# Packing the attention outputs of six head groups: an output projection with six products instead of eight

## The chip, the core and the metric

The kernel runs on one core of a Trainium2 chip. The metric is the device time of one execution in microseconds; less is better. The engines of the core are TensorE (PE, matrix products, with weight loads shown as PEld), VectorE (DVE), ScalarE (ACT), GpSimd (POOL) and SyncE (SP), which here mostly issues transfers.

## The reference

One transformer layer on a sequence of 2048 rows of 640 columns, in bf16: layer norm, attention with 32 heads of 20 columns each, an output projection with a residual, then layer norm and a bilinear gated feed-forward part of 1728 columns with a residual.

```
qkv = layernorm(x) @ wqkv                      # 640 -> 3 x 32 heads x 20
p   = softmax(q @ k.T * 20**-0.5)              # per head, 2048 x 2048
h   = x + concat_heads(p @ v) @ wo             # wo: 640 x 640
g   = layernorm(h) @ w_gate;  u = layernorm(h) @ w_up      # 640 -> 1728
out = h + (g * u) @ w_down
```

## The kernel before

**Layout.** The 32 heads are held in eight groups of four (NG = 8, HPG = 4). Each head has a slot of 32 partitions (SLOT), of which 20 hold its columns (DH) and one more, the 21st, the sum of its exponentials; so a group fills one tile of 128 partitions, with 80 useful rows. Queries and keys of group g stand in qa, qb and kT, values in vx. The 2048 query rows are worked in four blocks of 512 (QB). Block 0 is one pass over all keys ("0"); of blocks 1, 2 and 3 the first 4, 2 and 1 groups go in a full pass ("1", "2", "3") and the rest in two halves of 256 rows: "E" and "F", "C" and "D", "A" and "B".

**The main loop** goes through 683 score tiles of up to 1536 columns. emit_S computes the scores of a tile on TensorE (line 557) and has ScalarE take the exponential (line 573). From some tiles VectorE takes the last 512 columns instead, in four steps (emit_x, lines 610, 620, 621 and 615; tiles xv, xt, xe); ScalarE's call is then 1024 columns long. emit_AV multiplies the exponentials with the values (line 795) and, when a group is through, copies the sums to asb (line 807).

**From a group to its normed output.** norm sends the four rows of sums through DRAM (lines 666 and 667), takes the reciprocal (677), spreads it with transfers (682), and a step from the queue of VectorE's spare work, times, multiplies asb with it into the group's tile on (line 685, `On[g]`, one buffer per group). The multiplication for block b is held back until the output products of block b - 1 are in the order. The last groups of a pass (the set FAST) go a shorter way over TensorE instead (job_norm, lines 700 to 731).

**The output projection.** The weights wo are laid out like the outputs, with each head's 20 rows at the start of a 32-row slot and zeros between (load_wo, line 987 for the zeros, 991 for the loads, 32 of them). out_mm (line 1052) does for each row tile of 128 and each half of 320 columns eight products, one per group, then VectorE adds the residual (1056). The second layer norm follows (ln2_pieces, with its square root on GpSimd, lines 223 to 233), then the gated part (glu, 1203 to 1229) and the product with w_down (1270, 1274).

**The order** is written out by a planner when the kernel is built: generators for each job yield their cost, and the planner keeps clocks for TensorE, VectorE and ScalarE (at["pe"], at["dve"], at["exp"]) and lets jobs into the gaps between score tiles. PE_NS and ALONE_NS are the costs of whole jobs, which decide in the last block whether VectorE still takes exponentials (room). Where its account of TensorE's full-width work runs low it puts in idle products (keep_warm, line 508). No instruction moves afterwards; each engine works its list in order.

**The tail** (last_tail) handles the last 256 rows after the last exponential: for each row tile and half, out_most adds the residual and the products of seven groups (1376 and 1378), then the last group's norm is made on TensorE and VectorE (700 to 716, 1391), and out_last adds its product (1382). The second layer norm, the gated part and the last product follow.

A second path, general, works the whole thing again with maxima taken off, if a flag says that the exponentials' sums left their range. It doesn't run with these inputs.

Of the kernel before, what the change touches and what calls it, by code (L numbers as in the profile page):

```python
# [10 lines left out]
BF16 = mybir.dt.bfloat16  # L11
# [5 lines left out]
ALU = mybir.AluOpType  # L17
AX = mybir.AxisListType

P = 128  # L20
S = 2048
D = 640
# [17 lines left out]
FP = 7  # L40
FPW = 256
G1 = 4
SPLIT_G = {"1": 4, "2": 2, "3": 1}
QA = 3 * QB
RES0 = 3
# [24 lines left out]
FULL_IN, FULL_NS, ALL_NS = 2083, 300, 760  # L70
X_LEAST, X_OUT, X_SOON = 2, 5, 4
X_CHUNK = 3
PE_NS = {"out": 6000, "glu": 23000, "y": 7000}
NF_NS = 1800
ALONE_NS = {"out": 4350, "glu": 15260, "y": 5710}
PART_NS, TILE_NS, ROOM = 31500, 700, 2500
E_BUFS, E_LATE = 6, 2
SHIFT = 544.0
# [13 lines left out]
def kernel(  # L92
# [41 lines left out]
    shift_row = const.tile([P, 1], F32, name="shift_row")  # L134
    huge = const.tile([P, 1], F32, name="huge")
    half = const.tile([P, TPB], F32, name="half")
    wo = [const.tile([P, D], BF16, name=f"wo{g}") for g in range(NG)]
    N_SUMS = 16 * (NB * NG)
    sums_all = const.tile([P, N_SUMS], F32, name="sums_all")

# [2 lines left out]
    qsp = [dram.tile([P, S], BF16, name=f"qsp{g}", bufs=1) for g in range(NG)]  # L143
    kT = [qkp.tile([P, S], BF16, name=f"kT{g}") for g in range(NG)]
    vx = [vp.tile([P, VW], BF16, name=f"vx{t}") for t in range(NT)]
    On = [onp.tile([P, QB], BF16, name=f"on{g}") for g in range(NG)]

    lnT = ra.tile([P, KT, S], BF16, name="lnT")
    wv = [ra.tile([P, D], BF16, name=f"wv{c}") for c in range(KT)]
# [21 lines left out]
        nc.sync.dma_start(xs[0][:, t, :], x2d[t * P:(t + 1) * P, :])  # L171

    def wqk_half(c, hf):
        return (wo if hf else wqk)[c][:, 0:D].rearrange("p (m x) -> p m x", m=2)

    def load_wqk(hf):
        for c in range(KT):
# [478 lines left out]
    def read_out(b):  # L656
        return all(("om", b, t) in done for t in TAILS[b])

    def norm(s, asb):
        p, g = segs[s][0:2]  # L660
        b, c0, w = PASS[p]
        n = w // 32
        r16 = sums_all[:, col["n"]:col["n"] + n]
        col["n"] += n
        sums = dram.tile([HPG, w], F32, name="sums", tag=f"sums{w}")
        nc.sync.dma_start(sums[:], asb[DH:P:SLOT, 0:w])
        nc.sync.dma_start(r16, sums[:].rearrange("j (c f) -> (j c) f", f=n))

        due = at["dve"] + SUMS_NS

        def back():
            if at["pe"] < due and now["i"] < n_tiles:
                later(1, back)
                return
            ri = nrm.tile([P, n], F32, name="ri", tag=f"ri{n}")
            dve(130)
            nc.vector.reciprocal(ri[:], r16)  # L677
            scr = dram.tile([HPG, w], F32, name="scr", tag=f"scr{w}")
            nc.sync.dma_start(scr[:].rearrange("j (c f) -> (j c) f", f=n), ri[:])
            bc = nrm.tile([P, QB], F32, name="bc")  # L680
            for j in range(HPG):
                nc.sync.dma_start(bc[SLOT * j:SLOT * (j + 1), 0:w], scr[j:j + 1, :].to_broadcast([SLOT, w]))

            def times(asb, bc, p, g, c0, w):
                nc.vector.tensor_tensor(On[g][:, c0:c0 + w], asb[:, 0:w], bc[:, 0:w], ALU.mult)
                done.add(("n", p, g))
                yield 605 * w // QB

            def mult():
                if b and not read_out(b - 1):  # L690
                    later(1, mult)
                    return
                aux.append(times(asb, bc, p, g, c0, w))
            later(7, mult)
        later(4, back)
# [287 lines left out]
                add(("v", t, 1), job_V(t, 1))  # L983

    def load_wo():
        for g in range(NG):
            nc.vector.memset(wo[g][:], 0.0)
            yield 230
            for j in range(HPG):
                h = HPG * g + j  # L990
                nc.sync.dma_start(wo[g][SLOT * j:SLOT * j + DH, :], A_wo[DH * h:DH * h + DH, :])
            due = at["pe"] + WO_NS
            while at["pe"] < due and not now["forced"]:
                yield WAIT

    def make_identf():
        nc.vector.tensor_copy(identf[:], ident[:])
# [49 lines left out]
    def out_mm(on, st, t):  # L1047
        for hf in range(2):
            ps = bank()
            cs = slice(hf * HALF, (hf + 1) * HALF)  # L1050
            for g in range(NG):
                nc.tensor.matmul(ps[:, 0:HALF], lhsT=on[g][:, t * P:(t + 1) * P], rhs=wo[g][:, cs],  # L1052
                                 start=(g == 0), stop=(g == NG - 1))
                if g == NG - 1:
                    dve(408, 136)
                    nc.vector.tensor_tensor(st["h"][t][:, cs], ps[:, 0:HALF], st["xr"][t][:, cs], ALU.add)  # L1056
                yield 136
            done.add(("oh", t, hf))
            yield NEXT
# [306 lines left out]
    def last_tail():  # L1366
# [6 lines left out]
        def out_most(t, hf):  # L1373
            ps = ps_h[t, hf] = bank()
            cs = slice(hf * HALF, (hf + 1) * HALF)
            nc.tensor.matmul(ps[:, 0:HALF], lhsT=ident[:], rhs=st["xr"][t][:, cs], start=True, stop=False)
            for g in range(NG - 1):
                nc.tensor.matmul(ps[:, 0:HALF], lhsT=on[g][:, t * P:(t + 1) * P], rhs=wo[g][:, cs], start=False, stop=False)

        def out_last(t):  # L1380
            for hf in range(2):
                nc.tensor.matmul(ps_h[t, hf][:, 0:HALF], lhsT=on[NG - 1][:, t * P:(t + 1) * P],
                                 rhs=wo[NG - 1][:, hf * HALF:(hf + 1) * HALF], start=False, stop=True)
        ta, tb = LAST_T
        out_most(ta, 0)
        bc = sums_to_rows(sums_on_pe(asb, HW), HW)
# [128 lines left out]
    def general():  # L1515
        st = new_st(None)
        st["res"] = {}
        with tc.For_i(0, S, P) as r0:
# [3 lines left out]
            for g in range(NG):  # L1522
# [39 lines left out]
                nc.vector.tensor_tensor(oq[:, :, 0:DH], ov[:, :, 0:DH], ri[:].to_broadcast([P, HPG, DH]), ALU.mult)  # L1562
                ps = bank(BF16, P)
                nc.tensor.transpose(ps[:], oq[:].rearrange("p j e -> p (j e)"), ident[:])
                nc.vector.tensor_copy(On[g][:, 0:P], ps[:])
            for fn in (job_out(On, st, [0], None), job_glu(st, [0]), job_y(st, [0])):
                for _ in fn:
                    pass
# [33 lines left out]
```

## Time and profile before

| | |
|---|---|
| median of 3 runs | 896.7 us (895.01 to 898.06) |
| profiled execution: own time | 900.67 us |
| profiled execution: span | 898.8 us |
| mean granted TensorE clock | 0.989 |
| busy: TensorE, VectorE, ScalarE, GpSimd | 813.7, 773.7, 852.7, 31.4 us |
| output products before the tail (line 1052) | 224 matmuls, 41.6 us busy |
| output products in the tail (1378, 1382) | 28 and 4 matmuls |

In lines of the profile that are grouped, L1052 is line 1052 of the kernel; then come the engine, the operation, the tiles (out<-in), the count, the busy time, the mean in ns, and the engine's idle time just before with what ended it. Matmuls overlap, so their busy time is more than the time TensorE needs for them.

### The profile page before, as it was taken

How to read it: one execution, taken by the hardware profiler on the slowest of the kernel's cores; microseconds unless marked ns; L12 is line 12 of the kernel's file. 1: busy time of each engine (PE TensorE's matmuls, PEld its weight loads, DVE VectorE, ACT ScalarE, POOL GpSimd, SP SyncE). 2: the span in 40 equal slices, each digit the busy share in tenths (PEclk: the TensorE clock that was granted, in tenths of full speed). 3: DMA queues.
4: the chain of work that ended last, by engine and by line, in shares of the span. 5: the costliest groups of instructions: out<-in, count | busy, mean ns of one | idle time of the engine just before them, and what ended most of it. 6: DMA issues, size and time to landing. Idle time of an engine off the chain costs nothing.

```text
span 898.8 us, 21965 instructions
## 1 busy us (share of the span) xinstructions
PE 813.7 (91%) x8921; PEld 374.1 (42%) x8921; DVE 773.7 (86%) x1448; ACT 852.7 (95%) x719; POOL 31.4 (3%) x122
## 2 busy tenths in 40 slices
PE   7889999989999899889999998998899999999997
PEld 5333232222233344544444554443434455444465
DVE  7778899999999899789999998999889988889842
ACT  6999999999999999989999999999999999999951
POOL 4100000000002000001000000001000000000000
PEclk9999999999999999989999999999989999999999
DMA  6030010011034556432214334111441312010310
GB/s 198 25 65 2 1 28 25 15 36 28 14 84 112 122 146 198 112 88 66 54 51 122 81 96 107 47 30 29 121 121 45 85 31 74 15 44 9 94 38 18
DMA packets 110763, 60.15 MB, mean 67 GB/s; under 512 B 37976, under 2 KB 107652, under 8 KB 110656
## 3 DMA queue, kind: packets, MB, share of 16 engines
q1 hardware_dynamic: 110656, 58.68, 25.0%
q8 instruction: 72, 1.18, 0.6%
q14 instruction: 35, 0.29, 0.1%
HBM read 48.09 MB, written 7.28 MB: 62 GB/s over the span
## 4 chain that ended last, share of the span: by engine, by line
ACT 56%; PE 21%; issue 13%; DVE 9%; DMA 1%; SPq 0%; ACTq 0%; DVEq 0%
ACT E L573 46%; ACT El L573 10%; PE sc L557 5%; PE mi L1221 3%; PE acc L795 3%; PE f L1203 2%; PE mi L306 1%; PE mi L1052 1%; DVE xv L610 1%; PE mi L1270 1%; PE f L1270 1%; DVE xt L620 1%; DVE xt L621 1%; DVE xe L615 1%; DVE hh L1229 1%
## 5 line engine op out<-in xcount | busy, mean ns | idle before, releaser
L573 ACT ACTIVATE E<-sc 128x1536 bf16<-128x1536 f32 (+1 forms) x560 | 694.0, 1387 | 7.3 <-PE sc L557 6.0
L557 PE MATMUL sc<-qa,kT 32*128 32x256 bf16 (+1 forms) x2176 | 204.1, 320 | 23.8 <-ACT E L573 13.5
L557 PEld LDWEIGHTS <-kT 32*128 32x128 bf16 x3136 | 85.2, 92 | 223.9 <-issue 193.4
L610 DVE TENSOR_SCALAR xv<-sc 128x512 f32<-128x512 f32 x199 | 137.1, 690 | 47.3 <-PE sc L557 44.4
L573 ACT ACTIVATE El<-sc 128x1536 bf16<-128x1536 f32 (+1 forms) x123 | 159.7, 1371 | 0.6 <-PE sc L557 0.5
L795 PE MATMUL acc<-E,vx 128*32 128x256 bf16 (+1 forms) x2245 | 158.2, 315 | 0.6 <-DVE vx L271 0.6
L615 DVE SCALAR_TENSOR_TENSOR xe<-xt,xv 128x512 int16<-128x512 f32 x199 | 134.3, 681 | 0.8
L621 DVE SCALAR_TENSOR_TENSOR xt<-xt,xv 128x512 f32<-128x512 f32 x199 | 133.2, 680 | 0.6
L620 DVE SCALAR_TENSOR_TENSOR xt<-xv 128x512 f32<-128x512 uint16 x199 | 132.1, 679 | 0.3 <-DVE ri L677 0.2
L306 PE MATMUL mi<-lnT,wp 128*128 128x512 bf16 x305 | 86.5, 381 | 7.1 <-DVE qa L313 3.4
L795 PEld LDWEIGHTS <-vx 128*32 128x32 bf16 x3136 | 62.2, 96 | 62.5 <-issue 60.6
L557 PE MATMUL sc<-qb,kT 32*128 32x256 bf16 (+1 forms) x960 | 69.0, 283 | 3.4 <-ACT E L573 2.2
L1270 PE MATMUL mi<-wd,hh 128*128 128x320 bf16 x378 | 65.5, 301 | 1.1 <-DVE xr L1274 1.0
L1221 PE MATMUL mi<-ln2T,wg 128*128 128x256 bf16 x390 | 56.7, 274 | 8.6 <-DVE u L1226 7.2
L1221 PE MATMUL mi<-ln2T,wu 128*128 128x256 bf16 x390 | 55.5, 274 | 7.4 <-DVE hh L1229 7.2
L795 PE MATMUL acc<-El,vx 128*32 128x256 bf16 (+1 forms) x579 | 60.6, 294 | 0.5 <-ACT El L573 0.5
L795 PE MATMUL acc<-xe,vx 128*32 128x256 bf16 (+1 forms) x312 | 57.3, 306 | 0.0
L1270 PEld LDWEIGHTS <-hh 128*128 128x128 bf16 x448 | 37.9, 97 | 29.5 <-issue 18.2
L1221 PEld LDWEIGHTS <-wg 128*128 128x128 bf16 x390 | 33.6, 97 | 30.0 <-issue 25.3
L306 PEld LDWEIGHTS <-wp 128*128 128x128 bf16 x310 | 24.8, 97 | 50.6 <-issue 38.5
L1221 PEld LDWEIGHTS <-wu 128*128 128x128 bf16 x390 | 33.8, 97 | 28.3 <-issue 25.1
L1052 PE MATMUL mi<-wo,on 128*128 128x320 bf16 x224 | 41.6, 312 | 2.3 <-DVE xr L1056 2.2
(152 smaller groups left out, 623.0 us busy)
## 6 DMA issues: line engine op xcount, KB each, us to landing
wu<-in_B_w_up_dram SPq DMA_DIRECT2D x38, 320.0 KB
wg<-in_B_w_gate_dram SPq DMA_DIRECT2D x37, 320.0 KB
bc<-scr SPq DMA_DIRECT2D x60, 64.0 KB
bc<-scr SPq DMA_DIRECT2D x108, 32.0 KB
qsp<-qa SPq DMA_DIRECT2D x8, 384.0 KB
xr<-in_A_x_dram SPq DMA_DIRECT2D x16, 160.0 KB
out_dram<-xr SPq DMA_DIRECT2D x14, 160.0 KB
wd<-in_B_w_down_dram SPq DMA_DIRECT2D x13, 160.0 KB
```

The source lines that it names most:

```text
L306: nc.tensor.matmul(ps[:], lhsT=wslice(m, g, c), rhs=lnT[:, c, ch * QB:(ch + 1) * QB], start=(c == 0), stop=(c == KT - 1))
L557: nc.tensor.matmul(sc[:, o:o + w], lhsT=kT[g][SLOT * j:SLOT * (j + 1), kt * P:(kt + 1) * P], rhs=q_of(g, b, c0, w)[SLOT * j:SLOT * (j + 1) ...
L573: exps = nc.scalar.activation(e[:, 0:n_act], sc[:, 0:n_act], ACT.Exp, bias=EXP_BIAS, scale=SM_SCALE)
L610: took = nc.vector.tensor_scalar(v[:], ps, X_SCALE, X_BASE, ALU.mult, ALU.max)
L615: nc.vector.scalar_tensor_tensor(e[:], t[:], X_R, v[:], ALU.mult, ALU.add)
L620: lambda: nc.vector.scalar_tensor_tensor(t[:], u, X_P, u, ALU.add, ALU.mult),
L621: lambda: nc.vector.scalar_tensor_tensor(t[:], t[:], X_Q, u, ALU.add, ALU.mult),
L795: nc.tensor.matmul(acc["t"][SLOT * j:SLOT * (j + 1), 0:w], lhsT=vx[kt][:, VS * h:VS * h + SLOT], rhs=e, start=(acc["n"][j] == 0), stop=(ac ...
L1052: nc.tensor.matmul(ps[:, 0:HALF], lhsT=on[g][:, t * P:(t + 1) * P], rhs=wo[g][:, cs], start=(g == 0), stop=(g == NG - 1))
L1203: nc.tensor.matmul(ps[:, 0:n], lhsT=st["w", fp][k][:, c, f_cols(fp, f2)], rhs=st["ln2T"][:, c, c0:c0 + n], start=(c == 0), stop=(c == KT - 1))
L1221: nc.tensor.matmul(ps[:, f2 * n:(f2 + 1) * n], lhsT=st["w", fp][k][:, c, f_cols(fp, f2)], rhs=st["ln2T"][:, c, c0:c0 + n], start=(c == 0), ...
L1270: nc.tensor.matmul(ps[:, 0:HALF], lhsT=st["hh"][f // 2][:, f % 2, t * P % HW:t * P % HW + P], rhs=late["Wd"][f][:, cs], start=(f == 0), st ...
```

## The change

The 24 heads of groups 0 to 5 have 480 useful rows. They are packed into four dense tiles, d0 to d3, of 128, 128, 128 and 96 rows; groups 6 and 7 keep their padded tiles. So an output sum has six products instead of eight. The weights of the 24 heads are loaded dense, in four transfers. A product of groups 0 to 5 is now multiplied into a rotating tile (name on, two buffers), and pack copies it head by head into the dense tile with transfers issued by GpSimd; a head that crosses a tile's edge needs two. That is four or five transfers for each group and pass. Groups 6 and 7, which end last in each pass, are not packed. The planner's costs of an output job are lowered. In the changed kernel the lines stand a little further down: the pack's transfer is line 668, times 699, the output product 1017.

```diff
+PADDED = (6, 7)
+DENSE = ("d0", "d1", "d2", "d3")
+OUT_ROWS = {"d3": 96}
...
-PE_NS = {"out": 6000, "glu": 23000, "y": 7000}
+PE_NS = {"out": 4900, "glu": 23000, "y": 7000}
...
-ALONE_NS = {"out": 4350, "glu": 15260, "y": 5710}
+ALONE_NS = {"out": 3264, "glu": 15260, "y": 5710}
...
-    wo = [const.tile([P, D], BF16, name=f"wo{g}") for g in range(NG)]
+    wo = {k: const.tile([P, D], BF16, name=f"wo{k}") for k in DENSE + PADDED}
...
-    On = [onp.tile([P, QB], BF16, name=f"on{g}") for g in range(NG)]
+    On = {k: onp.tile([P, QB], BF16, name=f"on{k}") for k in DENSE + PADDED}
...
+    def pack(o, g, cols):
+        for j in range(HPG):
+            r, d = DH * (HPG * g + j), 0
+            while d < DH:
+                n = min(DH - d, P - (r + d) % P)
+                to = (r + d) % P
+                nc.gpsimd.dma_start(On[DENSE[(r + d) // P]][to:to + n, cols], o[SLOT * j + d:SLOT * j + d + n, cols])
+                d += n
...
             def times(asb, bc, p, g, c0, w):
-                nc.vector.tensor_tensor(On[g][:, c0:c0 + w], asb[:, 0:w], bc[:, 0:w], ALU.mult)
+                cols = slice(c0, c0 + w)
+                o = On[g] if g in PADDED else onp.tile([P, QB], BF16, name="on", bufs=2)
+                nc.vector.tensor_tensor(o[:, cols], asb[:, 0:w], bc[:, 0:w], ALU.mult)
+                if g not in PADDED:
+                    pack(o, g, cols)
...
     def load_wo():
-        for g in range(NG):
+        for k, key in enumerate(DENSE):
+            n = OUT_ROWS.get(key, P)
+            nc.sync.dma_start(wo[key][0:n, :], A_wo[P * k:P * k + n, :])
+        for g in PADDED:
...
+    def out_product(ps, key, t, cs, start, stop):
+        n = OUT_ROWS.get(key, P)
+        nc.tensor.matmul(ps[:, 0:HALF], lhsT=On[key][0:n, t * P:(t + 1) * P], rhs=wo[key][0:n, cs], start=start, stop=stop)
...
-            for g in range(NG):
-                nc.tensor.matmul(ps[:, 0:HALF], lhsT=on[g][:, t * P:(t + 1) * P], rhs=wo[g][:, cs],
-                                 start=(g == 0), stop=(g == NG - 1))
-                if g == NG - 1:
+            for key in DENSE + PADDED:
+                out_product(ps, key, t, cs, key == DENSE[0], key == PADDED[-1])
+                if key == PADDED[-1]:
...
-            for g in range(NG - 1):
-                nc.tensor.matmul(ps[:, 0:HALF], lhsT=on[g][:, t * P:(t + 1) * P], rhs=wo[g][:, cs], start=False, stop=False)
+            for key in (DENSE + PADDED)[:-1]:
+                out_product(ps, key, t, cs, False, False)
```

More of the change, by code (lines that the diff above doesn't have):

```diff
@@ L173, in wqk_half @@
     def wqk_half(c, hf):
-        return (wo if hf else wqk)[c][:, 0:D].rearrange("p (m x) -> p m x", m=2)
+        return (list(wo.values()) if hf else wqk)[c][:, 0:D].rearrange("p (m x) -> p m x", m=2)
     def load_wqk(hf):
@@ L1376, in out_most @@
             nc.tensor.matmul(ps[:, 0:HALF], lhsT=ident[:], rhs=st["xr"][t][:, cs], start=True, stop=False)
-            for g in range(NG - 1):
-                nc.tensor.matmul(ps[:, 0:HALF], lhsT=on[g][:, t * P:(t + 1) * P], rhs=wo[g][:, cs], start=False, stop=False)
+            for key in (DENSE + PADDED)[:-1]:
+                out_product(ps, key, t, cs, False, False)
         def out_last(t):
             for hf in range(2):
-                nc.tensor.matmul(ps_h[t, hf][:, 0:HALF], lhsT=on[NG - 1][:, t * P:(t + 1) * P],
-                                 rhs=wo[NG - 1][:, hf * HALF:(hf + 1) * HALF], start=False, stop=True)
+                out_product(ps_h[t, hf], NG - 1, t, slice(hf * HALF, (hf + 1) * HALF), False, True)
         ta, tb = LAST_T
@@ L1564, in general @@
                 nc.tensor.transpose(ps[:], oq[:].rearrange("p j e -> p (j e)"), ident[:])
-                nc.vector.tensor_copy(On[g][:, 0:P], ps[:])
+                o_t = On[g] if g in PADDED else onp.tile([P, QB], BF16, name="on", bufs=2)
+                nc.vector.tensor_copy(o_t[:, 0:P], ps[:])
+                if g not in PADDED:
+                    pack(o_t, g, slice(0, P))
             for fn in (job_out(On, st, [0], None), job_glu(st, [0]), job_y(st, [0])):
```

## The prediction

> **What bounds the kernel now.** I read the page first: the busy times of part 1 and the chain of part 4.
>
> ```profile
> PE 813.7 (91%) x8921; PEld 374.1 (42%) x8921; DVE 773.7 (86%) x1448; ACT 852.7 (95%) x719; POOL 31.4 (3%) x122
> ACT 56%; PE 21%; issue 13%; DVE 9%; DMA 1%; SPq 0%; ACTq 0%; DVEq 0%
> ```
>
> ScalarE carries 852.7 of 898.8 us and most of the chain: it is the bound, with TensorE and VectorE close behind. POOL is almost empty. Next I asked for busy time by stretches of 50 us (columns: stretch, its length, then busy us and count of PE, PEld, DVE, ACT, POOL, then granted clock, DMA share, GB/s).
>
> ```profile
> 250.00:300.00 50.00, 44.85 (x358) 15.69 (x358) 45.28 (x86) 49.41 (x42) 6.84 (x13) 0.97 0.41 105
> 300.00:350.00 50.00, 46.70 (x476) 21.44 (x474) 47.51 (x79) 50.00 (x43) 0.00 (x0) 1.00 0.55 144
> 350.00:400.00 50.00, 44.60 (x636) 24.25 (x638) 42.02 (x76) 49.39 (x41) 0.00 (x0) 0.97 0.48 139
> 400.00:450.00 50.00, 46.24 (x583) 21.76 (x580) 45.11 (x88) 47.70 (x41) 2.80 (x6) 0.96 0.22 56
> 650.00:700.00 50.00, 46.57 (x505) 21.12 (x505) 44.10 (x81) 48.37 (x41) 1.62 (x6) 0.93 0.37 98
> 700.00:750.00 50.00, 46.23 (x666) 25.23 (x658) 42.95 (x77) 49.86 (x42) 0.00 (x0) 1.00 0.23 57
> 850.00:899.00 49.00, 40.96 (x385) 29.54 (x379) 18.19 (x55) 18.70 (x31) 0.00 (x0) 0.97 0.09 26
> ```
>
> There are two stages. From about 25 to 858 us ScalarE has hardly a gap, and faster matmuls are worth nothing unless ScalarE waits for them. Where it waits, the granted clock is down: the four rows with clocks of 0.97, 0.97, 0.96 and 0.93 lack 0.59 + 0.61 + 2.30 + 1.63 = 5.1 us of ScalarE. From 858 us to the end TensorE is the chain.
>
> **The change, part by part.** *Exponentials.* The planner places work by its own costs, so I compared the order of the two built programs. VectorE takes 200 blocks of 512 columns instead of 199; one ScalarE call shrinks from 1536 to 1024 columns.
>
> ```profile
> L573 ACT ACTIVATE E<-sc 128x1536 bf16<-128x1536 f32 x397 | 561.3, 1511 | 4.5 <-PE sc L557 3.4 <-PE acc L795 0.4 <-ACT El L573 0.3
> L573 ACT ACTIVATE E<-sc 128x1024 bf16<-128x1024 f32 x163 | 171.7, 1082 | 2.8 <-PE sc L557 2.6 <-ACT E L573 0.2
> ```
>
> That is 1511 - 1082 = 429 ns: **-0.43 us**. The 683 calls otherwise stay.
>
> *Fewer output matmuls.* Sixteen row tiles, two halves and six products instead of eight take 64 matmuls away, 56 of them at L1052 before 858 us and 8 at L1378 in the tail. Chain, in order of time (start, us, what):
>
> ```profile
> 859.45 0.95 PE f L1378 x7
> 860.40 0.34 PE f L700 x4
> 860.89 0.95 PE f L1378 x7
> 861.84 0.44 PE acc L716 x4
> 863.37 0.27 PE f L1382 x2
> 863.78 0.95 PE f L1378 x7
> 864.73 0.27 PE f L1382 x2
> 865.00 1.90 PE f L1270 x14
> ```
>
> One such matmul takes 0.95/7 = 0.136 us of TensorE, so the 56 free 7.6 us under ScalarE's cover. Of this the chain gets nothing: the order shows ten more calls of keep_warm, and the one block above. If the cover were gone, they would be worth the 7.6.
>
> In the tail four groups of seven become groups of five, 0.27 us each. What is late next is VectorE:
>
> ```profile
> 859.24 0.42 DVE L807 COPY asb<-acc 128x256 f32<-128x256 f32 x1 [5.98 <-PE acc L795]
> 860.10 0.55 PEld L700 LDWEIGHTS f<-identf,asb 128*128 128x128 f32 x4
> 861.07 0.29 DVE L710 COPY bc<-ri 128x256 f32<-128x256 f32 x1
> 861.55 0.55 PEld L716 LDWEIGHTS acc<-identf,bc 128*128 128x128 f32 x4
> ```
>
> The first group's 0.27 is won whole: L700 could go from 859.66, when asb is copied. The second group's is mostly lost: bc ends at 861.36, after the first gain 861.09, so L716 goes from 861.55 to about 861.2, a gain of 0.35 and not 0.54. The third adds about 0.2 (the product L1391 comes just before), the fourth 0.27. Then the layer norm and everything behind it start **0.8 us** earlier; ends 0.5 and 1.09.
>
> *The packs.* Thirty-five groups' products go into a rotating tile and from there by 158 transfers, four or five each, into the dense tiles. No GpSimd transfer is in this trace, so its time on POOL (call it c) and until it lands must be bounded. Nearest rows: POOL's operations, SyncE's issue (min/median/max), and transfers of the sums in the chain.
>
> ```profile
> L198 POOL MEMSET vx<- 128x12 bf16 x16 | 2.6, 253 | 0.0
> L233 POOL TENSOR_TENSOR den<-v,half 128x2 bf16<-128x2 f32 (+1 forms) x9 | 8.2, 906 | 0.8
> L667 SPq DMA_DIRECT2D sums_all<-sums x42: 321/342/367, 114.4 to 841.2; - x42
> 693.13 1.60 DMA sums<-asb
> 371.04 4.34 DMA scr<-ri
> ```
>
> So c is 0.25 to 0.91 us and landing 1.6 to 4.3 us; I take 0.9, as descriptors written by a program are nearer to POOL's slowest row, and 1.6, since that row too leaves from SBUF. Landing matters only where a reader is near. In the built program six exponentials lie between block 1's last pack (F, group 5) and its output job, eight for E, twelve or more for C, D and A. Narrowest is the tail: the products of B, groups 4 and 5, stand behind exponentials 675 and 676, and 4 stood behind 670 before.
>
> ```profile
> 849.64 8.20 ACT L573 ACTIVATE E<-sc 128x1536 bf16<-128x1536 f32 x6
> 851.89 0.41 DVE L685 TENSOR_TENSOR on<-asb,bc 128x256 bf16<-128x256 f32 x1
> 859.28 1.11 PE L1378 MATMUL f<-wo,on 128*128 128x320 bf16 x7
> ```
>
> An exponential there takes 8.20/6 = 1.37 us; the product at 851.89 stood behind number 678, so the two will run near 847.8 and 849.1. Nine transfers must be issued and landed between 848.2 and the read of the last dense tile near 859.0 (0.43 earlier than now, three matmuls in): 10.8 us against 9 x 0.9 + 1.6 = 9.7. Hidden, by 1.1 us; at the upper ends (0.91 and 4.3) it is 1.7 late. For F: six times 1.37 is 8.2 us for 4 x 0.9 + 1.6 = 5.2, hidden.
>
> Behind a pack on POOL stand the steps of the second layer norm, up to the power whose result VectorE needs. In the built order each follows its pack by at least ten exponentials, or stands ahead of the pack, so I cost this at 0; if one were caught, the reciprocal would wait up to 5 x 0.9 = 4.5 us.
>
> The Trainium skill, "SBUF — State Buffer", section "SBUF: two separate sides", speaks against the change: while VectorE runs an SBUF-to-SBUF operation in a two-port mode, GpSimd can't write the descriptors of its transfers. The page "SBUF — State Buffer" gives 620 ns for one alone and 3100 ns beside such an operation; at 3.1 us, an estimate from that page, the tail would be some 19 us late. VectorE's rows say how often that mode could run:
>
> ```profile
> L615 DVE SCALAR_TENSOR_TENSOR xe<-xt,xv 128x512 int16<-128x512 f32 x199 | 134.3, 681 | 0.8
> L244 DVE TENSOR_SCALAR ln<-xr,m,rstd 128x640 bf16<-128x640 bf16 x14 | 5.8, 442 | 0.2
> ```
>
> The exponential's steps on VectorE take 681 ns for 512 columns, the normalisation 442 for 640: only the second looks like a fast mode, and it is 5.8 us in all. So I leave c where it was.
>
> *Waits.* An instruction carries two waits here; more become semaphore instructions of its engine.
>
> ```profile
> L685 DVEq EVENT_SEMAPHORE  x84: 21/35/50, 131.3 to 851.7; - x84
> L1052 PEldq EVENT_SEMAPHORE  x9: 51/51/51, 262.9 to 264.2; - x9
> L610 DVE TENSOR_SCALAR xv<-sc 128x512 f32<-128x512 f32 x199 | 137.1, 690 | 47.3 <-PE sc L557 44.4
> ```
>
> In the built program a packed product waits for eight or nine semaphores instead of four: 35 x 4.5 x 35 ns = 5.5 us of VectorE, which idles 47.3 us ahead of L610 waiting for scores; that covers it. The first products of an output job wait for some seven each: about 20 semaphore instructions of 51 ns, 1 us on TensorE's sequencer, in up to eight jobs. The scores of the next exponential are queued behind. The nine at 262.9 ran ahead of the matmuls and opened no gap on ScalarE. I take **+0.5 us** in all; ends 0 and 6.
>
> The output weights need 12 transfers instead of 32 and two memsets instead of eight, long before use: nothing. A dense tile is written again only after the previous block's products, which stand ahead in the order: nothing.
>
> **Sum**, against the profiled execution's own 900.67 us (898.8 of span, 1.9 around it): 900.67 - 0.43 - 0.80 + 0.50 = 899.9, 0.08% less. The median of the runs is 896.7, 0.4% under that execution: **896.0 us**. What a measurement can tell from no change is about 0.3%, 2.7 us.
>
> **Rivals.** *A, late packs: slower.* If c is over (10.8 - 1.6)/9 = 1.02 us, the tail waits on POOL: TensorE stands in order, so the sums' transposes behind the first output product wait too. At 1.4 us it is 9 x 1.4 + 1.6 - 10.8 = 3.4 us late, giving 899.4; at 2 us 8.8 in the tail and 1.4 in F's job, giving 906. For it: no row of a POOL transfer, and a memset of 12 columns already takes 253 ns. Against it: every row of POOL is under 0.91. Chance 0.25.
>
> *B, fewer waits at low clock: faster.* The 5.1 us of ScalarE above come and go with the clock. A shorter output job late in such a stretch, or a luckier order, could win them all: 890.9; half: 893.4. For it: the job at 401 us runs at half pace (the 400 to 450 row). [...] Chance 0.15.
>
> *C, more waits: slower.* With 64 full-width matmuls fewer, more stretches fall to the low clock, or the semaphore instructions show whole. Twice the 5.1 us gives 901.1. For it: scores come just in time. Against it: ten more keep_warm calls fill such holes. Chance 0.15. The Trainium skill, "TensorE: Matmul & The Clock Gate", section "What's actually happening", has the clock decided in free-running windows of about 3.4 us of TensorE activity; that would let these losses move from run to run, which one trace can't show.
>
> *The forecast*, packs hidden and as many waits as now: 0.45, with its own range 894 to 898. Faster by over 0.3%: B 0.13 and 0.06 of the forecast, 0.19. Slower: A 0.21, C 0.11 and 0.02 of the forecast, 0.34. Within: 0.47. The range, 892.5 to 903.5, takes in half of B, C, and A up to c of 1.8.
>
> **What would show it.** Right: 200 calls at the line of xv; the tail from the last exponential to the end 0.5 to 1.1 us shorter; no wait of TensorE for a dense tile; a POOL transfer under 1.02 us. Wrong: POOL still issuing packs at 859 us, TensorE waiting for them in the tail; a ScalarE gap at an output job that the clock doesn't explain; low-clock stretches other than the three or four rows above.

## The result, and the profile after

The changed kernel takes 904.87 us (median of 6 runs, 900.23 to 906.51) where the kernel before took 896.15 in the same comparison (895.01 to 898.38): a ratio of 1.0092, 95% interval 1.007 to 1.0113. It is slower by 8.7 us, outside the predicted range. The profiled execution took 906.51 us, with a span of 904.7. It and the profiled execution before (900.67) both had a mean granted clock of 0.989, and they differ by 5.8 us. Among 29 executions of the kernel before, beside e1, the time goes with the clock: 893.5 to 894.6 us at 0.999, 901.8 at 0.989, with a median clock of 0.996. The six of the changed kernel had 0.989 to 0.996, median 0.992. So the loss at equal clock is 5.8 us in this pair, and of the 8.7 the other 3 or so, an estimate from these two differences, go with a lower clock.

Two lines of the page, part 1 and the chain of part 4:

```profile
PE 803.3 (89%) x8817; PEld 370.9 (41%) x8874; DVE 774.6 (86%) x1446; ACT 853.8 (94%) x719; POOL 113.0 (12%) x280
ACT 50%; PE 23%; issue 13%; DVE 11%; DMA 2%; DVEq 0%; ACTq 0%
```

TensorE shows 10.4 us less work than before and GpSimd 82 us more. GpSimd's part was planned; TensorE's is in part missing records: the trace has 8817 matmuls to 8874 weight loads, where the kernel before has 8921 of each. ScalarE still has its 853 us to do, in a longer span. The same stretches of 50 us as before show where it stands idle (the first line is from the kernel before, whose other stretches stand in the prediction; the rest are the changed kernel's):

```profile
550.00:600.00 50.00, 46.32 (x644) 23.06 (x647) 44.96 (x84) 50.00 (x43) 0.00 (x0) 1.00 0.22 56
...
250.00:300.00 50.00, 42.88 (x331) 14.36 (x334) 44.56 (x85) 48.23 (x40) 6.31 (x16) 0.97 0.35 96
350.00:400.00 50.00, 42.89 (x611) 22.67 (x605) 42.99 (x75) 46.87 (x40) 7.12 (x14) 0.97 0.47 135
400.00:450.00 50.00, 44.40 (x617) 22.24 (x611) 45.51 (x89) 48.95 (x41) 7.64 (x15) 1.00 0.24 62
550.00:600.00 50.00, 45.67 (x620) 22.43 (x626) 43.31 (x81) 48.47 (x42) 4.56 (x9) 0.97 0.23 59
```

ScalarE, the fourth pair of each line, falls behind in three of them and gains in the stretch from 400 us. The rows of the exponentials carry the sum. Their last part is the idle time of ScalarE ahead of them, and what ended it. First the kernel before, the calls into E and into El, then the changed one:

```profile
L573 ACT ACTIVATE E<-sc 128x1536 bf16<-128x1536 f32 (+1 forms) x560 | 694.0, 1387 | 7.3 <-PE sc L557 6.0
L573 ACT ACTIVATE El<-sc 128x1536 bf16<-128x1536 f32 (+1 forms) x123 | 159.7, 1371 | 0.6 <-PE sc L557 0.5
```

```profile
L576 ACT ACTIVATE E<-sc 128x1536 bf16<-128x1536 f32 (+1 forms) x561 | 694.6, 1378 | 12.1 <-PE sc L560 11.2
L576 ACT ACTIVATE El<-sc 128x1536 bf16<-128x1536 f32 (+1 forms) x122 | 159.0, 1375 | 1.0 <-PE sc L560 0.7
```

Idle time grew from 7.9 to 13.1 us, nearly all of it waiting for TensorE's scores. The last exponential, which ended at 858.8 us before, now ends at 864.7. The chain in order of time (start, us, what), before and after, with the first long group of matmuls behind it:

```profile
857.62 1.15 ACT El L573
...
869.71 11.08 PE f L1203 x100
```

```profile
863.66 1.04 ACT E L576
...
875.09 11.08 PE f L1225 x100
```

That is 5.9 us, all of the difference between the two spans. So the loss is made in the stage that ScalarE bounds, in small waits for scores, and not in the tail.

The transfers themselves were cheaper than I took them (issue time in ns: min/median/max; the second line is us):

```profile
L668 POOL DMA_DIRECT2D ond<-on x158: 505/508/755, 132.8 to 859.3; - x158
DMA to landing us min/median/max: 1.5/2.3/5.0
```

And the semaphore instructions that the dense tiles bring to TensorE and VectorE:

```profile
L1017 PEldq EVENT_SEMAPHORE  x73: 51/51/51, 264.9 to 865.9; - x73
```

```profile
L699 DVEq EVENT_SEMAPHORE  x149: 21/50/50, 131.0 to 855.9; - x149
```

TensorE has 73 where the output products had 9. They don't lie spread out: in the built program the first product from a dense tile waits for up to eight semaphores, because the transfers into a tile go round eight DMA semaphores and the product waits for each. So they stand in bundles at the head of an output job. The first bundle, in the timeline of the changed kernel:

```profile
265.29 0.63 PE L1017 MATMUL mi<-wod,ond 128*128 128x320 bf16 x2
266.10 0.53 PE L1017 MATMUL mi<-wod,ond 128*128 128x320 bf16 x2 [0.18 <-issue]
266.47 0.48 PE L1017 MATMUL mi<-wo,on 128*128 128x320 bf16 x2
266.89 0.61 PE L560 MATMUL sc<-qa,kT 32*128 32x512 bf16 x3
267.60 1.02 ACT L576 ACTIVATE E<-sc 128x1024 bf16<-128x1024 f32 x1 [0.52 <-PE sc L560]
269.50 1.45 ACT L576 ACTIVATE E<-sc 128x1536 bf16<-128x1536 f32 x1 [0.88 <-PE sc L560]
```

From the first product to the scores behind the sixth it is 1.60 us (265.29 to 266.89), the scores then run at half clock (0.61 us instead of 0.39), and ScalarE idles 0.52 and 0.88 us for them. The last transfer into these tiles was issued by 200.6 us, so the data had landed long before: what holds TensorE up is its own wait instructions and, behind them, the half clock.

### The profile page after: what moved, and what is told of

Same layout as the page of the kernel before. It is cut to its first block, busy times and chain, and to the rows that moved or that the text cites. A ratio compares the mean times of both kernels' runs of the same rounds, so it can differ in the third digit from the quotient of the medians.

```text
span 904.7 us, 22134 instructions
## 1 busy us (share of the span) xinstructions
PE 803.3 (89%) x8817; PEld 370.9 (41%) x8874; DVE 774.6 (86%) x1446; ACT 853.8 (94%) x719; POOL 113.0 (12%) x280
## 4 chain that ended last, share of the span: by engine, by line
ACT 50%; PE 23%; issue 13%; DVE 11%; DMA 2%; DVEq 0%; ACTq 0%
ACT E L576 41%; ACT El L576 8%; PE sc L560 6%; PE mi L1243 4%; PE acc L811 4%; PE f L1225 2%; DVE xv L613 2%; PE mi L1017 2%; DVE xt L623 1%; DVE xt L624 1%; PE mi L511 1%; PE mi L309 1%; PE f L1292 1%; DVE hh L1251 1%; DVE xe L618 1%
## 5 line engine op out<-in xcount | busy, mean ns | idle before, releaser
L668 POOL DMA_DIRECT2D ond<-on x158 | 80.7, 518 | 490.9 <-DVE on L699 428.9
L309 PE MATMUL mi<-lnT,wp 128*128 128x512 bf16 x280 | 82.6, 381 | 8.7 <-DVE qa L316 3.4
L1243 PE MATMUL mi<-ln2T,wg 128*128 128x256 bf16 x410 | 60.1, 275 | 12.2 <-DVE u L1248 8.7
L1243 PE MATMUL mi<-ln2T,wu 128*128 128x256 bf16 x410 | 58.9, 274 | 9.0 <-DVE hh L1251 7.9
L811 PE MATMUL acc<-xe,vx 128*32 128x256 bf16 (+1 forms) x315 | 59.5, 308 | 0.3 <-issue 0.3
L1243 PEld LDWEIGHTS <-wg 128*128 128x128 bf16 x410 | 35.5, 98 | 35.3 <-issue 28.4
```

The costliest lines, as they stand in the source:

```text
L309: nc.tensor.matmul(ps[:], lhsT=wslice(m, g, c), rhs=lnT[:, c, ch * QB:(ch + 1) * QB], start=(c == 0), stop=(c == KT - 1))
L668: nc.gpsimd.dma_start(On[DENSE[(r + d) // P]][to:to + n, cols], o[SLOT * j + d:SLOT * j + d + n, cols])
L811: nc.tensor.matmul(acc["t"][SLOT * j:SLOT * (j + 1), 0:w], lhsT=vx[kt][:, VS * h:VS * h + SLOT], rhs=e, start=(acc["n"][j] == 0), stop=(ac ...
L1243: nc.tensor.matmul(ps[:, f2 * n:(f2 + 1) * n], lhsT=st["w", fp][k][:, c, f_cols(fp, f2)], rhs=st["ln2T"][:, c, c0:c0 + n], start=(c == 0), ...
```

## The experiments

The three theories of the first four: O, the planner's new order and the missing products make the loss; P, the transfers; W, the waits on TensorE's queue. Each kernel was timed in five rounds beside the kernel before; ratios are to that, as the comparison gives them, and can stand 0.2% off the quotient of the two medians. In e2, e5, e6, e9 and e15 the outputs of groups 4 and 5 are left out of the sum.

**e1_packs_only: the transfers alone.** The kernel before in its own order, with the 158 transfers added, into a tile that nobody reads.

```
                 nc.vector.tensor_tensor(On[g][:, c0:c0 + w], asb[:, 0:w], bc[:, 0:w], ALU.mult)
+                if g < 6:
+                    pack(On[g], g, slice(c0, c0 + w))
```

> The kernel before, in its own order on every engine, with the 158 pack transfers on GpSimd added; they copy into a spare tile that nobody reads, and the padded products stay eight. Theory O (the loss comes from the new order and the missing products, packs are innocent): 895 to 897 us, ratio 0.998 to 1.002. Theory P (the transfers themselves slow the rest: POOL beside VectorE, DMA queues, the longer waits of the multiplication on VectorE): 900 to 905 us. Theory W (waits on TensorE's queue ahead of the output products): 895 to 897, since nothing waits for these packs on TensorE.

Measured: 897.29 us, ratio 1.0012 (0.9991 to 1.0033). GpSimd's time is that of the changed kernel, 518 ns a transfer there and 516 here:

```profile
L669 POOL DMA_DIRECT2D ond<-on x158 | 80.4, 516 | 474.4 <-DVE on L698 445.6 <-DVE ri L690 14.5 <-DVE ri L723 11.4
```

The transfers cost nothing that can be told from no change. P falls, for the order of before.

**e2_six_no_packs: six products and a new plan, no transfers.** Groups 4 and 5 are left out of the output product, the planner is told the costs of six, and makes an order of its own.

```
...
-            for g in range(NG):
+            for g in USED:            # (0, 1, 2, 3, 6, 7)
...
```

> The kernel before without any pack, with the padded products of groups 4 and 5 left out (six products a sum, so the output lacks two head groups) and the changed planner's costs, so that the planner makes an order of its own for six products. Theory O: 902 to 906 us, as the changed kernel. Theories P and W: 894 to 896 us, a little under the kernel before.

Measured: 896.88 us, ratio 1.001 (0.9988 to 1.0031). Two products fewer and another order cost nothing and gain nothing, as predicted; P and W had expected a little less, 894 to 896.

**e3_old_order: the whole change in the order of before.** The planner keeps the costs of eight products, finds two empty turns in each half tile, and loads the output weights in eight turns as before.

```
...
-            for key in DENSE + PADDED:
-                out_product(...)
+            for key in DENSE + (None, None) + PADDED:
+                if key is not None:
+                    out_product(...)
```

> The changed kernel whole (dense tiles, packs on GpSimd, six products and their waits), but with the planner's costs and yields as for eight products, so that every engine's order is that of the kernel before and TensorE has holes where two products were. Theory O, if the order alone is to blame: 894 to 897 us; if the missing products (TensorE idle, low clock) are to blame: 900 to 905. Theories P and W: 902 to 905 us.

Measured: 898.92 us, ratio 1.0031 (1.0012 to 1.0051). The same 73 waits, with the transfers, cost 0.3% here (0.1 to 0.5), a third of the loss. That is above what O expected of the order (894 to 897) and below what P and W expected (902 to 905).

**e4_sync_packs: SyncE issues the transfers.** The changed kernel's order.

```
-                nc.gpsimd.dma_start(On[DENSE[...]]...)
+                nc.sync.dma_start(On[DENSE[...]]...)
```

> The changed kernel with its own order, the packs issued by SyncE instead of GpSimd. Theory O: 903 to 906 us as the changed kernel. Theory P, if POOL beside VectorE costs: 896 to 899 us; if the number of transfers and waits costs: 904 or more. Theory W: 903 to 906, the waits stay.

Measured: 925.85 us, ratio 1.0328 (1.0296 to 1.0361), far above every range. Issue on SyncE takes longer, and the transposes and the sums' round trips of other groups stand behind it:

```profile
L668 SPq DMA_DIRECT2D ond<-on x158: 554/713/1670, 136.1 to 878.9; - x158
```

```profile
298.60 2.10 PE L1243 MATMUL mi<-ln2T,wu 128*128 128x256 bf16 x9 [2.24 <-DMA ln2T<-ln]
301.35 2.79 ACT L576 ACTIVATE E<-sc 128x1536 bf16<-128x1536 f32 x2 [3.24 <-PE sc L560]
```

In the timeline (second fence) TensorE waits 2.24 us for a transposed tile and ScalarE pays 3.24. Of the two, GpSimd is the right queue for the transfers. What the four runs leave open is why the changed kernel's own order loses 8.7 us when neither transfers nor order alone do. The next three runs ask that; theory X says that this order has no room for the waits.

**e5_order_alone: the changed kernel's order, no transfers.** The order of ScalarE, VectorE and TensorE is that of the changed kernel, instruction for instruction; products read the padded tiles of groups 0 to 3, 6 and 7.

```
-                o = On[g] if g in PADDED else onp.tile([P, QB], BF16, name="on", bufs=2)
+                o = On[DENSE[g] if g < 4 else g]
...
-                if g not in PADDED:
-                    pack(o, g, cols)
```

> The changed kernel's own order on ScalarE, VectorE and TensorE, instruction for instruction, with no packs: every group keeps a padded tile of its own, and the six products of a half tile read the padded tiles of groups 0 to 3, 6 and 7 (the outputs of groups 4 and 5 are left out). So no product waits for a pack. Theory O (the order that the planner made for six products is itself the slower one): 903 to 906 us, with the half-clock stretches near 267, 396, 584, 604 and 850 us still there and some 5 us more ScalarE gaps than before. Theory W (the waits for the packed tiles on TensorE's queue make the loss, in whatever order): 896 to 898 us. Theory X (the order has no slack, so that waits which the old order absorbs cost 6 us in it): 896 to 899 us here too, and only e7 tells it from W.

Measured: 897.37 us, ratio 1.0004 (0.9984 to 1.0024). The order alone is not slower. O falls.

**e6_order_packs: the same with the transfers, into a tile that nobody reads.**

```
+    Dn = {k: spare for k in DENSE}
...
-                nc.gpsimd.dma_start(On[DENSE[...]]...)
+                nc.gpsimd.dma_start(Dn[DENSE[...]]...)
```

> As e5_order_alone, and the 158 small transfers by GpSimd go as in the changed kernel, but into one spare tile that no product reads (groups 4 and 5 left out of the product). So GpSimd's and the DMA engines' work is that of the change, and no product waits for it. Theory O: 903 to 906 us, as e5. Theory W and theory X: 896 to 899 us, within 1.5 us of e5; if it stands 4 us or more above e5, the transfers themselves delay this order (by the DMA queues or the port that GpSimd shares), which e1 in the old order did not show.

Measured: 897.84 us, ratio 1.0004 (0.9985 to 1.0023). Order and transfers together cost nothing that can be told from no change. What the changed kernel has beyond this is that its products read what the transfers wrote. Since the order is the same, instruction can be set beside instruction. The first output job of e6:

```profile
263.37 7.48 ACT L576 ACTIVATE E<-sc 128x1536 bf16<-128x1536 f32 x6
...
265.37 0.72 PE L1019 MATMUL mi<-wod,ond 128*128 128x320 bf16 x4
...
265.93 0.44 PE L1019 MATMUL mi<-wo,on 128*128 128x320 bf16 x2
266.29 0.39 PE L560 MATMUL sc<-qa,kT 32*128 32x512 bf16 x3
```

Here the scores follow 0.92 us behind the first product, not 1.60, at full clock, and ScalarE runs six calls without a gap. The changed kernel's exponentials start 0.2 us ahead of e6's up to this job and 2.0 behind it; by the last exponential they are 6.7 behind.

**e7_whole_other_order: the whole change in the order of e2.** Only the turns that the loading of the output weights takes in VectorE's plan differ.

```
-        for g in PADDED:
-            nc.vector.memset(wo[g][:], 0.0)
+        for g in range(NG):
+            if g in PADDED:
+                nc.vector.memset(wo[g][:], 0.0)
             yield 230
...
```

> The changed kernel whole (packs, dense tiles, six products, planned for six), but its loading of the output weights takes eight turns of VectorE's plan instead of two, as before, which gives the order of e2_six_no_packs on ScalarE and TensorE, instruction for instruction. e2 took 896.9 us without packs and waits. Theory O: 896 to 899 us (e2 and some 1 to 2 us of waits, as between before and e3). Theory W: 902 to 906 us. Theory X: between, 899 to 903 us, as the order of e2 has no holes where two products were.

Measured: 899.83 us, ratio 1.0035 (1.0019 to 1.0051). In the gap between what O and W expected, as X had it. It has the 73 waits:

```profile
L1019 PEldq EVENT_SEMAPHORE  x73: 51/51/51, 262.9 to 860.8; - x73
```

**e8_collector: the waits moved off TensorE.** The changed kernel whole, in its own order; GpSimd copies the packed columns of a row tile into tiles that the products read, so that GpSimd holds the waits for DMA semaphores and TensorE waits for GpSimd alone.

```
+    def collect(t):                       # ahead of the products of row tile t
+        for key in DENSE:
+            nc.gpsimd.tensor_copy(Read[key][..., tile t], On[key][..., tile t])
...
-        nc.tensor.matmul(..., lhsT=On[key][...], ...)
+        nc.tensor.matmul(..., lhsT=Read[key][...], ...)
```

> The changed kernel whole, in its own order on ScalarE, VectorE and TensorE, but for each tile of 128 rows GpSimd copies the four packed tiles' columns (64 small copies) into tiles that the products read. So GpSimd waits for the transfers, on up to eight DMA semaphores a tile, and TensorE waits for one semaphore of GpSimd instead. In the changed kernel's trace TensorE's queue holds 11 waits, 0.11 us apart, ahead of the first half tile of an output job (265.08 to 266.48 us), and against e6_order_packs, which has the same order, ScalarE loses 2.2 us there and 6.7 us in all, in steps. Theory W (these bundles of waits make the loss, with the half-clock stretches that follow them): 896 to 900 us, the bundle at 265 us gone and the first six products done in 0.8 us instead of 1.8. Theory T (it is the transfers as sources of the products, their landing or the reading of tiles that DMA wrote): 902 to 906 us, as the changed kernel.

Measured: 898.07 us, ratio 1.0023 (1.001 to 1.0036). The products' line and ScalarE's row:

```profile
L1024 PEldq EVENT_SEMAPHORE  x4: 51/51/51, 265.1 to 448.9; - x4
```

```profile
L576 ACT ACTIVATE E<-sc 128x1536 bf16<-128x1536 f32 (+1 forms) x561 | 693.6, 1384 | 7.8 <-PE sc L560 7.3 <-PE acc L818 0.4
```

With 4 semaphore instructions instead of 73, and the order and the transfers of the changed kernel, 0.69% of its 0.92% are gone, 6.2 us.

**e9_waits_alone: e6 with the waits put back.** Four tiny products of 8 columns, whose results nobody reads, read the spare tiles ahead of an output job.

```
+            for key in DENSE:
+                nc.tensor.matmul(ps[:, HALF:HALF + 8], lhsT=Dn[key][...], rhs=ident[..., 0:8], ...)
```

> e6_order_packs (the changed kernel's order, transfers into spare tiles, six products of padded tiles, groups 4 and 5 left out) with the waits put back: ahead of the first product of an output job TensorE makes four tiny products of 8 columns that read the four spare tiles, whose results nobody reads. They carry the bundle of waits for DMA semaphores that the changed kernel's products carry, and cost some 0.1 us each themselves. e6 took 897.8 us. Theory W: 901 to 906 us, with a bundle of 10 or more waits near 265 us and a ScalarE gap of 0.5 us or more behind it. Theory T: 897 to 899 us.

Measured: 907.85 us, ratio 1.0142 (1.0127 to 1.0157), 10 us over e6 by the medians and 12 by the ratios, and above W's range (901 to 906). Its four runs had clocks of 0.984 to 0.989, e6's twelve 0.989 to 0.998; at 0.989 one execution of e9 took 904.65 us and one of e6 900.71. So at equal clock it is some 4 us, and the rest goes with the lower clock. Its rows:

```profile
L670 PEldq EVENT_SEMAPHORE  x70: 51/51/51, 264.5 to 863.7; - x70
```

```profile
268.14 1.02 ACT L576 ACTIVATE E<-sc 128x1024 bf16<-128x1024 f32 x1 [1.46 <-PE sc L560]
```

```profile
L576 ACT ACTIVATE E<-sc 128x1536 bf16<-128x1536 f32 (+1 forms) x561 | 693.8, 1380 | 10.6 <-PE sc L560 9.8 <-PE acc L823 0.4
```

The bundles bring the loss back in a kernel whose own six products wait for no transfer. No run has the 28 tiny products without the waits, so their share is not known. Together with e8: in this order the waits are the cause. Taken away the loss goes, put back it comes.

**e10_other_collector: the same remedy in e7's order.** The edit is that of e8, in e7.

> e7_whole_other_order (the changed kernel whole, in the order of e2, 899.8 us) with the copies by GpSimd of e8, so that its products wait for one semaphore of GpSimd. Theory W: 896 to 898.5 us, near e2 (896.9, without packs). Theory T: 899 to 901 us, as e7.

Measured: 901.14 us, ratio 1.0063 (1.0047 to 1.008): a miss for W, no better than e7. One place explains part of it:

```profile
776.40 0.57 POOL L1136 TENSOR_TENSOR den<-v,half 128x1 bf16<-128x1 f32 x1 [13.77 <-DVE mb L1138]
776.94 2.04 POOL L676 COPY rdd<-ond 128x128 bf16<-128x128 bf16 x4
777.37 0.31 PE L1026 MATMUL mi<-wod,rdd 128*128 128x320 bf16 x1 [0.87 <-POOL rdd L676]
...
779.79 1.45 ACT L576 ACTIVATE El<-sc 128x1536 bf16<-128x1536 f32 x1 [2.00 <-PE sc L560]
```

The copies of a second row tile stand on GpSimd behind a step of the layer norm that VectorE releases late, TensorE waits for them, and ScalarE for TensorE: a new wait in the place of the old one.

**e11_first_block and e12_other_blocks: a part of the waits.** The copies of e8 for the first block alone, and for all blocks but the first.

```
+        n_out[0] += 1
+        via = n_out[0] <= 4          # e11; > 4 in e12
+        lhsT=(Read if via else On)[key]
```

> The changed kernel with GpSimd's copies (as in e8_collector) for the first block alone; the later blocks' products wait for the transfers themselves, as in the changed kernel. e8, with the copies for all blocks, took 898.1 us, the changed kernel 904.9. If the bundles of waits add up, each with the half-clock stretch it brings, the first block's share goes: against e6 the changed kernel's ScalarE lost 2.2 of 6.7 us at the first block's bundle (265 to 270 us), and another 1.8 up to 391 us in waits for DMA round trips. So 901 to 903 us. If one bundle is enough for the whole loss (a delay that the later schedule carries on), 897 to 899 us.

> The reverse of e11_first_block: the first block's products wait for the transfers themselves, those of the later blocks read GpSimd's copies. If the bundles add up: 900 to 903 us, with the bundle at 265 us and none later; the two losses, of e11 and of this, over e8 should sum to about the changed kernel's 6.8 us. If the first block's bundle is enough: 903 to 905 us; if it does nothing: 897 to 899 us.

Measured: e11 902.2 us, ratio 1.0056 (1.0033 to 1.0079); e12 903.92, ratio 1.0072 (1.0049 to 1.0096), beside a before of 897.3. Over e8's 1.0023 the later blocks' bundles cost 0.33%, the first block's 0.49%, together 0.82%; the whole is 0.69% (1.0092 less 1.0023). So they add up, within intervals of 0.2% each. But they don't go by the number of waits:

```profile
L1026 PEldq EVENT_SEMAPHORE  x61: 51/51/51, 264.5 to 860.9; - x61
```

```profile
L1026 PEldq EVENT_SEMAPHORE  x16: 51/51/51, 265.2 to 452.6; - x16
```

Sixteen waits (e12, second row) cost no less, as far as the intervals tell, than sixty-one (e11). e11 lies in the range that adding up had, e12 0.9 us above it.

The two traces with the same first bundle say more. Fifteen waits stand at 264.9 to 266.5 us in the changed kernel and at 265.2 to 266.8 in e12. The stretch from 265 to 270.5 us, with e6 (2 waits) first, then e12, then the changed kernel (ScalarE is the fourth pair, the clock follows the fifth):

```profile
265.00:270.50 5.50, 5.46 (x48) 2.16 (x47) 5.22 (x11) 5.50 (x5) 0.00 (x0) 1.00 0.59 153
265.00:270.50 5.50, 5.03 (x42) 1.89 (x42) 4.50 (x10) 5.14 (x6) 0.00 (x0) 1.00 0.54 154
265.00:270.50 5.50, 5.25 (x31) 1.59 (x29) 3.38 (x7) 4.09 (x4) 0.00 (x0) 0.69 0.55 155
```

At full clock the bundle costs ScalarE 0.36 us, with the half clock behind it 1.41. In e12 the clock falls at 296.6 us instead, and ScalarE idles 2.20 us there:

```profile
299.54 2.79 ACT L576 ACTIVATE E<-sc 128x1536 bf16<-128x1536 f32 x2 [2.20 <-PE sc L560]
```

So the waits alone are the smaller part at this place, and the half clock behind them the larger. The changed kernel and e9 have it there, e12 not. In the 3.41 us ahead of the fall TensorE was busy 2.21 us in the changed kernel (263.29 to 266.70) and 1.93 in e9 (262.59 to 266.00); the clock is half in the 3.41 us that follow. That the idle time between the waits brings the fall is a reading; no run isolates it.

**e13_other_early and e14_early: the copies in one go.** So that no copy stands behind a layer-norm step, all columns of a pass are copied right behind its last transfers, in e7's order (e13) and in the changed kernel's (e14).

```
+        if len(got) == NG - len(PADDED):
+            nc.gpsimd.tensor_copy(Read[key][..., ready columns], On[key][..., ready columns])
```

> e7_whole_other_order (899.8 us) with GpSimd's copies, but all columns in one go right behind the last transfers of a pass (28 copies), so that no copy stands behind a step of the layer norm on GpSimd. In e10 the copies of a second row tile stood behind such a step (776.40 us), TensorE waited for them 1.7 us in all, and ScalarE 2.0 at 779.8; up to 527 us e10's trace was 3.9 us ahead of e7's. Theory W (the bundles of waits cost in this order too, and e10 only lost the gain again to its own copies): 896 to 898.5 us, no wait of TensorE for a copy. If the bundles cost nothing in this order: 899 to 901 us.

> The changed kernel whole in its own order with the copies of e13, in one go behind the last transfers of a pass. Theory W: 896 to 898.5 us, at or below e8 (898.1), near e5 and e6 (897.4 and 897.8), which have the same order without the change's waits. If the place of the copies matters otherwise (GpSimd's layer-norm steps held up behind them), 899 us or more.

Measured: e13 900.95 us, ratio 1.0052 (1.0031 to 1.0072); e14 898.14, ratio 1.0017 (0.9998 to 1.0036). In the changed kernel's own order the remedy holds a second time. In e7's it fails a second time, in the range for "the bundles cost nothing in this order", and its trace shows another price of the copies:

```profile
199.59 3.18 DVE L623 SCALAR_TENSOR_TENSOR xt<-xv 128x512 f32<-128x512 uint16 x1
199.95 2.27 POOL L680 COPY rdd<-ond 128x512 bf16<-128x512 bf16 x4
...
203.86 1.45 ACT L576 ACTIVATE E<-sc 128x1536 bf16<-128x1536 f32 x1 [1.13 <-PE sc L560]
```

A step of VectorE that takes 0.68 us elsewhere takes 3.18 beside GpSimd's four copies, and ScalarE idles 1.13 for it. So e10 and e13 added costs of their own, and don't settle e7's order.

**e15_other_unread: e6 in e7's order.** No copies and no bundles; the transfers go where nobody reads.

> e6_order_packs in the order of e7_whole_other_order: the 158 transfers go into one spare tile that no product reads, the six products read padded tiles, and groups 4 and 5 are left out. So the bundles of waits are away without any copies by GpSimd (in e13 a VectorE step beside the copies took 3.18 us instead of 0.68, at 199.59 us, so e13 and e10 took one cost away and added another). e2, without transfers, took 896.9; e7, the whole change in this order, 899.8. Theory W (the bundles cost in this order too): 896.5 to 898 us. If it is something else in the change (transfers, VectorE's waits): 899 to 900.5 us.

Measured: 898.88 us, ratio 1.0036 (1.0022 to 1.005): the same as e7, 1.0035, which has the bundles. It lies just below what "something else" had expected, and above W's range. In this order the 73 waits cost nothing that shows. What e7 has over e2 (1.001, an interval that nearly reaches it) is there without them.

## Why the prediction was wrong

*The exponentials*: right. VectorE took 200 blocks, with steps of 682 to 690 ns as before. The first of the four:

```profile
L613 DVE TENSOR_SCALAR xv<-sc 128x512 f32<-128x512 f32 x200 | 137.9, 690 | 52.2 <-PE sc L560 49.8
```

*Fewer matmuls under cover*: right. They are worth nothing; e2, e5 and e6 stand at 1.001 and 1.0004.

*The tail*: half right. From the last exponential to the first long group of matmuls it was 10.94 us (858.77 to 869.71) and is 10.39 (864.70 to 875.09): 0.55 won, not 0.80. From there to the end it is 29.6 us instead of 29.1, most of that in what follows the last product, so the whole tail came out the same, 40.0 us, and the sign that I had named (0.5 to 1.1 us shorter to the end) did not come.

*The packs, and rival A*: c is 0.51 us where I took 0.9, from a slow POOL row, and landing 2.3 where I took 1.6. Nine transfers in the tail:

```profile
855.30 4.55 POOL L668 DMA_DIRECT2D ond<-on  x9 [22.36 <-DVE on L699]
...
865.42 0.84 PE L1017 MATMUL f<-wod,ond 128*128 128x320 bf16 x4
```

All are issued by 859.85, 5.6 us ahead of the first reader. A, which had most of the chance of slower, did not happen. The rule of the Trainium skill that I had weighed against the change ("SBUF — State Buffer", section "SBUF: two separate sides": GpSimd locked out of writing descriptors while VectorE runs in a two-port mode) did not show here: the slowest of 158 issues took 755 ns.

*Waits*: here the prediction failed, in the term that I put at +0.5 us with ends 0 and 6. I had the mechanism, "the scores of the next exponential are queued behind", and the count, about 20 in up to eight jobs (15 at most in the trace). What was wrong was the step from there: the nine waits at 262.9 us in the kernel before "ran ahead of the matmuls and opened no gap on ScalarE", so I took the bundles as nearly covered. Nine waits that no exponential felt are no measure of fifteen, nor of what comes behind them: at full clock fifteen cost ScalarE 0.36 us (e12), with a half-clock stretch behind them 1.41, and the delay then grew at later places. I also priced one at its duration, 51 ns; in the first bundle fifteen lie between 264.9 and 266.5 us, with five weight loads among them, some 0.11 us each. In this order the term of 0.5 measures 6.2 us (e8), and 4 (at equal clock) to 10 (by the medians) in e9.

*Rival C*, "the semaphore instructions show whole", was the nearest, at 901.1 and a chance of 0.15. That its number came close is luck: it was worked out from the low clock alone, not from the waits. More low clock is not what sets the changed kernel apart in the profiled executions: the granted clock over the whole run is the same as in e8, whose span is 6.1 us shorter (the changed kernel's first):

```profile
core 0: 904.7 us, clock 0.989
```

```profile
core 0: 898.6 us, clock 0.988
```

Half-clock stretches stand beside many of ScalarE's gaps, the first bundle's among them. Their total doesn't decide between these two; where they fall may, as e12 shows at the first bundle. Rival B stayed away in the sum: ScalarE won 1.3 us in the stretch from 400 us and 1.6 in that from 650, and lost more elsewhere.

What stays open: why the same 73 waits cost some 6 us in one order and nothing measurable in the other. The gaps right behind the bundles sum to some 2 us in the changed kernel's trace; the rest of the 6.7 us against e6 comes later, in steps of 0.3 to 0.7 us, often where TensorE or VectorE wait for a DMA round trip (296.8, 385.9 and 443.2 us). That the order of the changed kernel has less slack at those places is my reading; no run isolates it.

## What to carry to other kernels

A tile that many small transfers fill is paid for by its reader: each transfer's semaphore can become a wait instruction on the reading engine's own queue, even when the data landed long ago. Count them ahead of the first reader, price each at its pitch in the queue and not its duration, and look what stands behind the bundle in that engine's order. What they cost depends on that order: here 6 us in one and nothing in another. If the reader's engine feeds the bound, let an idle engine take the waits, with its copies placed where nothing late stands ahead of them, or fill the tile with fewer transfers (which no run here tries).

## What the runs showed of the hardware

- A transfer of 4 to 20 rows of 256 or 512 columns takes GpSimd 0.51 us to issue (505 to 755 ns) and 2.3 us to land; SyncE takes 0.71 us for the same (554 to 1670).
- Beside GpSimd's copies from SBUF to SBUF a VectorE step stood for 3.18 us instead of 0.68, 2.5 us more for 2.27 us of copies. The Trainium skill, "SBUF — State Buffer", section "SBUF: two separate sides", has the port pair of the two engines as an exclusive lock, held for a whole instruction, also against a VectorE step with two SBUF inputs; this trace agrees that the step stood until the copies were through, and it was the four together that held it up, not one. It differs on who holds the pair: by the page it is the instruction that starts first, and here the step's record begins 0.36 us ahead of the first copy's.
- Wait instructions of 51 ns in a bundle follow each other at some 0.11 us on TensorE's queue (fifteen from 264.9 to 266.5 us), with everything that they wait for landed long before.
- The granted clock falls to half in stretches (0.50 from 266.70 to 270.11 us in the changed kernel), here right behind a bundle of fifteen waits. Behind the same bundle in e12 it did not: 1.00 over 265 to 270.5 us, against 0.69.
